# First batch's attention and the first weight tiles in another order: linear attention and a low-rank mixer on one NeuronCore

## The chip, the cores and the metric

The kernel runs on one core of a Trainium2 chip. The metric is the device time of one execution in microseconds (us), the median of five runs. A profile is one more execution, recorded by the hardware profiler; its times are counted from its first instruction. The engines are named as in the profile: PE is TensorE's products, PEld its weight loads, DVE is VectorE, ACT is ScalarE, POOL is GpSimd, SP is the engine that issues the DMAs.

## The reference

Attention with a decaying state, for 4 batches, 8 heads, 768 steps and a head of 48; then a mixer over its output, which mixes the steps through rank 32 and the channels through a two-layer network (384 to 1536 to 384).

```python
f = 1.0 / (1.0 + np.exp(-f_logit))
for t in range(S):
    state = f[:, :, t, :, None] * state + np.einsum('bhd,bhe->bhde', k[:, :, t], v[:, :, t])
    y[:, :, t] = np.einsum('bhd,bhde->bhe', q[:, :, t], state)
...
x = y.transpose(0, 2, 1, 3).reshape(B, S, H * D)
h = x.transpose(0, 2, 1) @ U @ V
u = x + h.transpose(0, 2, 1)
out = u + np.maximum(u @ w_ch1, 0.0) @ w_ch2
```

The weights U, V, w_ch1 and w_ch2 arrive as 64-bit floats, the rest as 32-bit.

## The kernel before

**Units of attention.** A unit is two heads of one batch; there are 16, four to a batch. The sequence of a unit is cut into 12 chunks of 64 steps. `prepare(n)` makes the front of unit n: `gates` (transposes of the forget gates on TensorE into PSUM, L506, and the sigmoid on ScalarE, L527 and L528), `keep` (a backward running product `X` on VectorE, L540, and small follow-ups L545 to L550), `keys` (transposes of k, and `kz` = k times `X`, L518), `read_back` (a forward scan `Y`, L558) and `queries` (the same for q). After each tensor is used, the load of that tensor for unit n + 2 is issued on SP (`follow`, L394).

`attend(n)` makes the rear: `kept` transposes `kz` back (L610) and copies it to `kb` on ScalarE (L614); `states` copies each chunk's whole decay to a broadcast tile `whole` (L618), multiplies `kb` with v into the PSUM tile `ds` (L626) and copies that, interleaved, into `added` (L632); `scan` adds the states up over the chunks on VectorE (L641), in place in `added`, and for batches after the first copies the sums on to a tile `st` (L648); `scores` makes the products of q and k (L589) and masks them into `A` (L596); `read` multiplies q with the states into `y` (L661) and then has ScalarE copy two numbers of it to `seen` (L668), which orders what follows behind it; `inner` adds the products of `A` and v (L679) and copies `y` to `x` (L685). `whole` and `kb` have one buffer each, `st` two, the PSUM tiles of attention share three (`ps_big`).

**The mixer of the first batch.** `low_rank` makes x times U (L146) and a copy `h` (L149); `added_up` sums its four parts (L154) and copies them again (L156); `mix` multiplies with V into `pu` (L171), and VectorE adds the result to x (L161), three additions of 128x768; `turn(a)` transposes a third of x into `put` (L181) and copies it to `uT` (L182). Then `ch1` makes the first layer's products, six groups of 12 records for each pair of weight tiles (`pz`, L193, copied through a Relu at L200); `ch2`, and from the second batch `seven`, the second layer's (L215, L238).

**The weights.** Each tile is loaded raw by SP (L55) and turned from 64 to 32 bits: two copies on ScalarE (L64, L65), three operations on VectorE (L66, L67, L68), one addition on POOL (L69). The list `loads` holds U, two pieces of V (`early` is 3), twelve tiles of w_ch1 and twelve of w_ch2, in this order; the w_ch1 tiles go into `w`, two of them to a pair of `pz` groups.

**What sets the order.** TensorE's instructions stand in the order of the program's calls throughout (L745), VectorE's and ScalarE's as long as the first batch's mixer runs (L746); behind that a planner places those of VectorE and ScalarE, and scans, masks and additions have a high priority there. [...] The four units of batch 0 are written out by hand at L755 to L790. `busy(n)` puts n idle products (L753), whose result nobody reads, into TensorE's list: two at the start, three in each unit, and one before each of the first three pieces of the mixer (`idles`, L780). After the fourth unit's pieces, U and the first piece of V are converted, then unit 3's reading and inner products are done, then V's second piece and the first two tiles of w_ch1. In the mixer one entry of `loads` follows each piece, except the pieces 1 and 2 (`added_up` and `mix`), so the third tile stands behind `low_rank`.

```python
pieces += rear(n - 1, "read") + rear(n, "states", "scan", "scores") + rear(n - 1, "inner")
...
idles = {0: 1, 1: 1, 2: 1}
...
if loads and i not in (1, 2):
    loads.pop(0)()
```

Of the kernel before, what the change touches and what calls it, by code (L numbers as in the profile page):

```python
# [10 lines left out]
F32 = mybir.dt.float32  # L11
# [4 lines left out]
ALU = mybir.AluOpType  # L16
# [307 lines left out]
def factored_path(ctx, tc, q, k, v, f_logit, moe_U, moe_V, moe_w_ch1, moe_w_ch2, out, ok):  # L324
# [4 lines left out]
    nc = tc.nc  # L329
    B, H, S, D = q.shape  # L330
    P = nc.NUM_PARTITIONS
    C = P // 2
    NCH = S // C

    NBL = S // P
    HP = H // 2
# [18 lines left out]
    one = ctx.enter_context(tc.tile_pool(name="one", bufs=1))  # L355
# [215 lines left out]
    def attend(n):  # L571

        b, hp = divmod(n, HP)
        T = units[n]
        vt = v_tiles[n]
        rows = [slice(par * PAD, par * PAD + D) for par in range(2)]
        chunk = [slice(c * C, (c + 1) * C) for c in range(NCH)]

        part = [slice(s * C, (s + 1) * C) for s in range(2)]

        def scores():


            T["A"] = two.tile([P, 2, NBL, C], F32, name="A")
            sc = ps_big.tile([P, 2, 512], F32, name="sc", tag="big")
            for c in range(NBL):
                for par in range(2):
                    for s in range(2):
                        nc.tensor.matmul(  # L589
                            sc[part[s ^ par], par, c * C : (c + 1) * C],  # L590
                            lhsT=T["k"][rows[par], chunk[2 * c + s]],
                            rhs=T["q"][rows[par], chunk[2 * c + s]],
                            start=True, stop=True,
                        )
            with tc.high_priority(offset=AHEAD):
                nc.vector.tensor_tensor(  # L596
                    T["A"],
                    sc[:, :, 0 : NBL * C].rearrange("p h (c i) -> p h c i", i=C),
                    causal.unsqueeze(1).unsqueeze(1).broadcast_to((P, 2, NBL, C)),
                    ALU.mult,  # L600
                )

        def kept():

            pt = ps_big.tile([P, 2, 512], F32, name="pt", tag="big")
            for c in range(NBL):
                for par in range(2):
                    r = slice(par * PAD, (par + 1) * PAD)
                    o = c * P + (1 - par) * C
                    nc.tensor.transpose(  # L610
                        pt[:, par, c * PAD : (c + 1) * PAD], kz[n % 2][r, o : o + P], ident[r, r]
                    )
            kb = T["kb"] = one.tile([P, 2, NBL, PAD], F32, name="kb")
            nc.scalar.copy(kb.rearrange("p h c d -> p h (c d)"), pt[:, :, 0 : NBL * PAD])  # L614

        def states():
            whole = T["whole"] = one.tile([P, D, NCH], F32, name="whole")
            nc.scalar.copy(whole, wholes[n % 2].unsqueeze(1).broadcast_to((P, D, NCH)))  # L618

            ds = ps_big.tile([P, 2, 512], F32, name="ds", tag="big")  # L620
            for c in range(NBL):
                for s in range(2):
                    for par in range(2):

                        i = (c + (s & par)) % NBL
                        nc.tensor.matmul(  # L626
                            ds[par * PAD : (par + 1) * PAD, s, c * D : (c + 1) * D],
                            lhsT=T["kb"][part[s ^ par], par, i, :], rhs=vt[part[s ^ par], c, par, :],
                            start=True, stop=True,
                        )  # L630

            nc.scalar.copy(  # L632
                added[:, 1:].rearrange("p (e c s) -> p e c s", c=NBL, s=2),
                ds[:, :, 0 : NBL * D].rearrange("p s (c e) -> p e c s", e=D),
            )

        def scan():

            states = added[:, 0 : D * NCH]
            with tc.high_priority(offset=AHEAD):  # L640
                nc.vector.tensor_tensor_scan(  # L641
                    states, states, T["whole"].rearrange("p e c -> p (e c)"), 0.0, ALU.add, ALU.mult
                )
                T["st"] = states.rearrange("p (e c) -> p c e", c=NCH)
                if b > 0:

                    st = two.tile([P, NCH, D], F32, name="st")
                    nc.scalar.copy(st, T["st"])  # L648
                    T["st"] = st

        def read():


            y = T["y"] = ps_big.tile([P, 2, 512], F32, name="y", tag="big")

            def o(s, par, c):
                return y[part[s], par, c * D : (c + 1) * D]

            for c in range(1, NCH):
                for par in range(2):  # L660
                    nc.tensor.matmul(  # L661
                        o(c % 2, par, c // 2), lhsT=T["q"][rows[par], chunk[c]], rhs=T["st"][rows[par], c, :],
                        start=(c <= 2), stop=False, skip_group_check=True,
                    )


            seen = two.tile([P, 2], F32, name="seen")
            nc.scalar.copy(seen, y[:, :, (NBL - 1) * D])  # L668

        def inner():  # L670
            y = T["y"]

            def o(s, par, c):
                return y[part[s], par, c * D : (c + 1) * D]

            for c in reversed(range(NBL)):
                for par in range(2):
                    for s in range(2):
                        nc.tensor.matmul(  # L679
                            o(s, par, c), lhsT=T["A"][part[s ^ par], par, c, :], rhs=vt[part[s ^ par], c, par, :],  # L680
                            start=False, stop=True, skip_group_check=True,
                        )
            if hp == 0:
                x_tiles[b] = two.tile([P, NBL, DM], F32, name="x")
            nc.scalar.copy(  # L685
                x_tiles[b].rearrange("p c (h d) -> p h c d", d=D)[:, 2 * hp : 2 * hp + 2],
                y[:, :, 0 : NBL * D].rearrange("p h (c d) -> p h c d", d=D),
            )
            del units[n], v_tiles[n]

        return [kept, states, scan, scores, read, inner]
# [54 lines left out]
    with tc.manual_schedule(engines={nc.vector.engine, nc.scalar.engine}):  # L746


        idle = ps_mm.tile([P, 512], F32, name="idle", tag="mm")

        def busy(n):
            for _ in range(n):
                nc.tensor.matmul(idle[:, 0:DM], lhsT=ident, rhs=ends[:, 0:DM], start=True, stop=True)  # L753

        busy(2)  # L755
        for piece in front(0, "gates"):
            piece()
        for n in range(HP):
            pieces = front(n, "keep", "keys") + rear(n - 1, "scan", "scores")
            pieces += [lambda: busy(3)] + rear(n, "kept") + front(n, "read_back", "queries")  # L760
            if n + 1 < HP:
                pieces += front(n + 1, "gates") + rear(n - 1, "read", "inner") + rear(n, "states")
            else:
                pieces += rear(n - 1, "read") + rear(n, "states", "scan", "scores") + rear(n - 1, "inner")
            for piece in pieces:
                piece()
            if n < 2:
                load(n + 2, "v")
            if n == 1:

                loads = ahead_by(early + FIRST, weights)
            elif n > 1:
                load(n + 2, "f", "k", "q", "v")
        for piece in loads[:2] + rear(HP - 1, "read", "inner") + loads[2 : early + 2]:
            piece()
        loads = loads[early + 2 :]

        m = mixer(0)
        start = m.before[:5] + m.firsts[0:1] + m.before[5:]
        idles = {0: 1, 1: 1, 2: 1}  # L780

        EARLY = 9
        second = chain(front(HP, "gates", "keep", "keys", "read_back", "queries"), steps(HP, 2 * HP + 1))
        for i, (_, piece) in enumerate(start + m.firsts[1:]):
            busy(idles.get(i, 0))
            piece()
            if loads and i not in (1, 2):
                loads.pop(0)()
            if i >= EARLY:
                next(second)()  # L790
        for f in loads:
            f()
        n = len(m.seconds) // (NBL // 2)
        todo, after = m.seconds[:-n], m.seconds[-n:]

        attention(second, 12 + 10 * HP - (len(start) + len(m.firsts) - 1 - EARLY), todo)
        m = start_mixer(1, after)
        for f in to_sum:
            f()
# [343 lines left out]
```

## Time and profile before

| | us |
|---|---|
| median of five runs | 503.35 |
| lowest and highest | 502.57, 505.9 |
| the profiled execution's own time | 503.69 |
| its span, first to last instruction | 501.9 |
| TensorE products busy in it | 485.9 (97%) |
| VectorE, ScalarE, POOL busy | 274.8, 157.2, 37.6 |
| mean granted TensorE clock | 0.992 |

The page of the profile gives each engine's busy time in 40 equal slices of 12.5 us, in tenths:

```profile
PE   6897999999999999999999999999999999999995
DVE  5895989787587757656865436633411431222232
ACT  2424665664333313423332222413311122101010
PEclk9997999999999999999999999999999999999999
```

TensorE is below nine tenths in the first three slices and in the last, and the granted clock is below full in the fourth. The median of a group of instructions, and what an engine waited for, come from the groups and waits of the same trace; a wait marked "issue" is one for which the profile shows no releaser. Where a matmul ends is modelled.

### The profile page before, as it was taken

The numbers are of one execution on the slowest core, as the hardware profiler recorded it, in microseconds if no ns is written. First come the engines' busy times: TensorE is split into PE (matmuls) and PEld (weight loads), VectorE is DVE, ScalarE is ACT, GpSimd is POOL, SyncE is SP. The second block draws the span as 40 slices with busy tenths as digits, with TensorE's granted clock in tenths as the row PEclk, the third lists the DMA queues.
The fourth block names the chain that finished last, engine by engine and source line by source line (L and its number), as shares of the span: only waits on it lengthen the run. The fifth ranks groups of instructions, "written<-read, shape, count | busy, mean of one in ns | idle before, by whom it ended". The sixth has DMA issues, their size and how long they took to land.

```text
span 501.9 us, 12045 instructions
## 1 busy us (share of the span) xinstructions
PE 485.9 (97%) x5319; PEld 405.3 (81%) x5319; DVE 274.8 (55%) x396; ACT 157.2 (31%) x297; POOL 37.6 (7%) x49
## 2 busy tenths in 40 slices
PE   6897999999999999999999999999999999999995
PEld 4676588887666568898898888898899888999995
DVE  5895989787587757656865436633411431222232
ACT  2424665664333313423332222413311122101010
POOL 3000345442000000000000000000000000000000
PEclk9997999999999999999999999999999999999999
DMA  9979977634676422424534100100000000000001
GB/s 145 153 165 241 210 177 174 175 88 62 102 110 102 91 39 28 66 29 88 65 50 80 25 31 3 25 1 34 2 3 31 2 33 1 0 33 0 31 3 39
DMA packets 149269, 34.32 MB, mean 68 GB/s; under 512 B 139798, under 2 KB 147670, under 8 KB 149206
## 3 DMA queue, kind: packets, MB, share of 16 engines
q1 hardware_dynamic: 149206, 33.44, 35.5%
q8 instruction: 44, 0.72, 0.7%
q14 instruction: 19, 0.16, 0.1%
HBM read 28.70 MB, written 4.72 MB: 67 GB/s over the span
## 4 chain that ended last, share of the span: by engine, by line
PE 92%; SPq 3%; DVE 2%; DMA 1%; issue 1%; ACT 0%; ACTq 0%
PE pz L193 38%; PE pw L238 25%; PE po L215 10%; PE y L679 3%; PE y L661 3%; PE pt L506 3%; PE sc L589 3%; PE ds L626 2%; SPq L394 2%; PE put L181 2%; PE pt L610 1%; DMA f_raw<-in_f_logit_dram 1%; PE idle L753 1%; PE pu L171 1%; PE ph L146 1%
## 5 line engine op out<-in xcount | busy, mean ns | idle before, releaser
L193 PE MATMUL pz<-uT,w 128*128 128x256 f32 x864 | 195.8, 382 | 0.1
L193 PEld LDWEIGHTS pz<-uT,w 128*128 128x128 f32 x864 | 161.1, 190 | 22.1 <-issue 0.3
L200 ACT ACTIVATE z<-pz 128x512 f32<-128x512 f32 x63 | 37.6, 596 | 131.7 <-PE pz L193 127.5
L238 PE MATMUL pw<-w,z 128*128 128x192 f32 x324 | 56.5, 329 | 0.4 <-DVE o L161 0.4
L238 PE MATMUL pw<-zw,w_raw 128*128 128x192 f32 x324 | 55.9, 327 | 0.0
L238 PEld LDWEIGHTS pw<-w,z 128*128 128x128 f32 x324 | 52.8, 190 | 2.3 <-DVE o L161 1.6
L238 PEld LDWEIGHTS pw<-zw,w_raw 128*128 128x128 f32 x324 | 53.0, 190 | 1.3 <-DVE o L161 1.2
L161 DVE TENSOR_TENSOR w_raw<-z 128x768 f32<-128x768 f32 x18 | 17.2, 954 | 56.3 <-ACT z L200 56.3
L69 POOL TENSOR_TENSOR w<-w_y,w_r 128x384 int32<-128x384 int32 x24 | 31.5, 1311 | 35.9 <-DVE w_y L68 28.0
L540 DVE TENSOR_TENSOR_SCAN X<-fz,ends 128x768 f32<-128x768 f32 x16 | 28.1, 1756 | 10.5 <-ACT fz L527 6.2
L558 DVE TENSOR_TENSOR_SCAN Y<-fz,starts 128x768 f32<-128x768 f32 x16 | 27.9, 1746 | 0.2
L641 DVE TENSOR_TENSOR_SCAN added<-added,whole 128x576 f32<-128x576 f32 x16 | 21.6, 1352 | 8.8 <-ACT added L632 8.8
L215 PE MATMUL po<-w,zw 128*128 128x384 f32 x72 | 25.6, 499 | 0.0
L215 PE MATMUL po<-w,z 128*128 128x384 f32 x72 | 25.3, 495 | 0.0
L596 DVE TENSOR_TENSOR A<-sc,causal 128x768 f32<-128x768 f32 x16 | 15.2, 947 | 16.9 <-PE sc L589 16.9
L161 DVE TENSOR_TENSOR w_y<-x,pw 128x192 f32<-128x192 f32 x9 | 3.2, 354 | 38.5 <-ACT w_y L251 38.5
L648 ACT COPY st<-added 128x576 f32<-128x576 f32 x12 | 14.7, 1222 | 18.9 <-DVE added L641 18.9
L161 DVE TENSOR_TENSOR w_y<-w_y,pw 128x192 f32<-128x192 f32 x18 | 6.2, 347 | 25.6 <-PE pw L238 25.6
L215 PEld LDWEIGHTS po<-w,zw 128*128 128x128 f32 x72 | 12.9, 189 | 8.7 <-issue 1.2
L614 ACT COPY kb<-pt 128x768 f32<-128x768 f32 x16 | 12.7, 795 | 22.0 <-PE pt L610 22.0
L215 PEld LDWEIGHTS po<-w,z 128*128 128x128 f32 x72 | 13.0, 190 | 8.1 <-DVE o L161 0.6
L66 DVE TENSOR_SCALAR w_y<-w_y 128x384 f32<-128x384 f32 (+3 forms) x27 | 13.1, 484 | 11.6 <-ACT w_y L64 11.4
(102 smaller groups left out, 533.1 us busy)
## 6 DMA issues: line engine op xcount, KB each, us to landing
w_raw<-in_moe_w_ch_dram SPq DMA_DIRECT2D x18, 384.0 KB, 3.6
out_dram<-o SPq DMA_DIRECT2D x24, 192.0 KB, 2.0
f_raw<-in_f_logit_dram SPq DMA_DIRECT2D x16, 144.0 KB, 4.6
k_raw<-in_k_dram SPq DMA_DIRECT2D x16, 144.0 KB, 4.2
q_raw<-in_q_dram SPq DMA_DIRECT2D x16, 144.0 KB, 4.2
v_nat<-in_v_dram SPq DMA_DIRECT2D x16, 144.0 KB, 4.2
v_nat<-in_v_dram SPq DMA_DIRECT2D x32, 72.0 KB, 2.8
zw<-in_moe_w_ch_dram SPq DMA_DIRECT2D x6, 384.0 KB, 7.3
```

The source lines that it names most:

```text
L69: nc.gpsimd.tensor_tensor(dst.bitcast(I32), shaped(y.bitcast(I32)), shaped(r), ALU.add)
L161: nc.vector.tensor_tensor(*args)
L193: nc.tensor.matmul(pm[:, i * 2 * P : (i + 1) * 2 * P], lhsT=w1[:, m, o : o + P], rhs=uT[a][:, m, :], start=(m == 0), stop=(m == NDC - 1))
L200: nc.scalar.activation(z[a, c][:, k : k + 2, :].rearrange("p i t -> p (i t)"), pm, AF.Relu)
L215: nc.tensor.matmul(pm, lhsT=z[a, i // NI][:, i % NI, s * P : (s + 1) * P], rhs=w2[:, i, :], start=(i == 0), stop=(i == NFC - 1))
L238: nc.tensor.matmul(pm[:, n * HM : (n + 1) * HM], lhsT=lhs[:, i, :], rhs=rhs[:, i, :], start=(i == 0), stop=(i == NI - 1))
L506: nc.tensor.transpose(pt[:, 2 * c // NBL, c % (NBL // 2) * P : (c % (NBL // 2) + 1) * P], nat[n % 2][nm][:, c].rearrange("p h d -> p (h d) ...
L540: nc.vector.tensor_tensor_scan(backwards(X, S - 1, S), backwards(f, S, S), backwards(ends, S - 1, S), 0.0, ALU.mult, ALU.add,)
L558: nc.vector.tensor_tensor_scan(Y, f[:, 0:S], starts, 0.0, ALU.mult, ALU.add)
L589: nc.tensor.matmul(sc[part[s ^ par], par, c * C : (c + 1) * C], lhsT=T["k"][rows[par], chunk[2 * c + s]], rhs=T["q"][rows[par], chunk[2 * ...
L596: nc.vector.tensor_tensor(T["A"], sc[:, :, 0 : NBL * C].rearrange("p h (c i) -> p h c i", i=C), causal.unsqueeze(1).unsqueeze(1).broadcast ...
L641: nc.vector.tensor_tensor_scan(states, states, T["whole"].rearrange("p e c -> p (e c)"), 0.0, ALU.add, ALU.mult)
```

## The change

Six edits, all in the part of the program that handles the first batch, except that the order of two copies and the place where `st` is made hold for every unit:

1. One idle product at the start in place of two.
2. The copy to `whole` moves from `states` to `kept`, ahead of the copy to `kb`.
3. In the first batch the scan writes a tile `st` with two buffers instead of writing over `added`; TensorE reads the states from there, with the same strides. Later batches still scan in place and copy to `st`.
4. In the last unit of the first batch `states` comes ahead of the reading of the unit before.
5. Behind it, unit 3's reading comes ahead of the conversion of U and V's first piece.
6. No idle product before `low_rank`; and the third tile of w_ch1 is converted behind `mix` instead of behind `low_rank`.

```diff
                         pt[:, par, c * PAD : (c + 1) * PAD], kz[n % 2][r, o : o + P], ident[r, r]
                     )
+            whole = T["whole"] = one.tile([P, D, NCH], F32, name="whole")
+            nc.scalar.copy(whole, wholes[n % 2].unsqueeze(1).broadcast_to((P, D, NCH)))
             kb = T["kb"] = one.tile([P, 2, NBL, PAD], F32, name="kb")
             nc.scalar.copy(kb.rearrange("p h c d -> p h (c d)"), pt[:, :, 0 : NBL * PAD])
 
         def states():
-            whole = T["whole"] = one.tile([P, D, NCH], F32, name="whole")
-            nc.scalar.copy(whole, wholes[n % 2].unsqueeze(1).broadcast_to((P, D, NCH)))
...
         def scan():
 
-            states = added[:, 0 : D * NCH]
+            st = T["st"] = two.tile([P, NCH, D], F32, name="st")
+            by_e = "p (e c) -> p c e"
+            if b == 0:
+                states = st.rearrange("p c e -> p (c e)")
+                T["st"] = states.rearrange(by_e, c=NCH)
+            else:
+                states = added[:, 0 : D * NCH]
             with tc.high_priority(offset=AHEAD):
                 nc.vector.tensor_tensor_scan(
-                    states, states, T["whole"].rearrange("p e c -> p (e c)"), 0.0, ALU.add, ALU.mult
+                    states, added[:, 0 : D * NCH], T["whole"].rearrange("p e c -> p (e c)"), 0.0, ALU.add, ALU.mult
                 )
-                T["st"] = states.rearrange("p (e c) -> p c e", c=NCH)
                 if b > 0:
 
-                    st = two.tile([P, NCH, D], F32, name="st")
-                    nc.scalar.copy(st, T["st"])
-                    T["st"] = st
+                    nc.scalar.copy(st, states.rearrange(by_e, c=NCH))
...
-        busy(2)
+        busy(1)
...
-                pieces += rear(n - 1, "read") + rear(n, "states", "scan", "scores") + rear(n - 1, "inner")
+                pieces += rear(n, "states") + rear(n - 1, "read") + rear(n, "scan", "scores") + rear(n - 1, "inner")
...
-        for piece in loads[:2] + rear(HP - 1, "read", "inner") + loads[2 : early + 2]:
+        for piece in rear(HP - 1, "read") + loads[:2] + rear(HP - 1, "inner") + loads[2 : early + 2]:
             piece()
...
-        idles = {0: 1, 1: 1, 2: 1}
+        idles = {1: 1, 2: 1}
...
-            if loads and i not in (1, 2):
+            if loads and i > 1:
                 loads.pop(0)()
```

## The prediction

> **What bounds the kernel now.** I read the busy table by stretch first, then the chain of waits, then the timeline of the first 58 us. The stretches (columns: us of the stretch, busy us and instructions of each engine, granted TensorE clock, DMA share, GB/s):
>
> ```profile
> core 0: us, PE busy (x) PEld busy (x) DVE busy (x) ACT busy (x) POOL busy (x), PEclk, DMA share, GB/s
> 0.00:20.05 20.05, 14.43 (x173) 9.85 (x173) 13.74 (x20) 6.35 (x12) 4.66 (x22) 1.00 1.25 152
> 20.05:38.31 18.26, 17.61 (x448) 13.51 (x448) 15.88 (x19) 7.21 (x16) 0.00 (x0) 1.00 0.82 162
> 38.31:42.65 4.34, 2.18 (x105) 2.04 (x105) 2.45 (x3) 1.54 (x4) 0.00 (x0) 1.00 1.06 344
> 42.65:58.00 15.35, 13.59 (x221) 8.60 (x220) 11.33 (x22) 7.30 (x19) 4.47 (x6) 0.78 1.04 165
> 58.00:496.44 438.44, 438.04 (x4375) 371.30 (x4375) 231.07 (x333) 134.84 (x248) 28.49 (x21) 1.00 0.28 55
> ```
>
> From 58 us TensorE is full for 438.04 of 438.44 us. So the change can pay or cost only before its first `pz` product (57.99), and a shift there reaches the end whole. Before it TensorE idles 10 us, under three different limits.
>
> Until 20.05 it is the loads. Unit 2's forget gates land at 19.91, as SP issues 0.4 to 1 us per DMA and the engines are full:
>
> ```profile
> 14.53 5.38 DMA f_raw<-in_f_logit_dram
> ```
>
> Then, 20.05 to 40.5, it is TensorE and VectorE in turn. Then TensorE stops for 2.16 us in the middle of the scores of unit 3, where no semaphore stands ("issue"), and its clock halves:
>
> ```profile
> 42.65 0.86 PE L589 MATMUL sc<-qT,kz 48*64 48x64 f32 x35 [2.16 <-issue]
> ...
> q8 instruction: 1, 0.02, 2.3%
> ...
> 42.60:46.60 4.00, 3.39 (x128) 3.23 (x127) 1.61 (x4) 1.63 (x6) 0.00 (x0) 0.57 1.01 175
> ...
> 43.00:43.50 0.50, 0.50 (x36) 0.50 (x32) 0.00 (x0) 0.00 (x0) 0.00 (x0) 0.63 1.34 227
> ...
> 49.50:50.00 0.50, 0.50 (x5) 0.20 (x8) 0.47 (x3) 0.50 (x2) 0.00 (x0) 0.54 1.19 159
> ```
>
> These are from the timeline, from the DMA queues of the stretch 39.5 to 42.5 (one packet of instructions; in 35.5 to 40 there is none) and from the table by stretch. Its last two lines show the clock leaving 1.00 near 43.1 and returning near 50.0. The rest, to 58, is a thin chain:
>
> ```profile
> 46.42 0.14 ACT L668 COPY seen<-y 128x2 f32<-128x2 f32 x1
> ...
> 46.64 1.53 PE L679 MATMUL y<-v_nat,A 64*64 64x48 f32 x48 [0.59 <-ACT seen L668]
> ...
> 50.53 0.57 ACT L64 ACTIVATE w_y<-zw 128x384 f32<-128x384 f32 x1 [0.34 <-POOL V L69]
> ...
> 51.97 0.91 PE L154 MATMUL ph<-h,blocks 128*128 128x384 f32 x2
> ...
> 52.95 0.55 ACT L65 ACTIVATE w_r<-zw 128x384 int32<-128x384 uint32 x1
> ...
> 53.40 0.47 ACT L156 COPY h<-ph 128x384 f32<-128x384 f32 x1
> ...
> 54.01 1.56 PE L171 MATMUL pu<-h,V 32*128 32x384 f32 x12 [0.48 <-ACT h L156]
> ...
> 54.65 0.56 DVE L68 SCALAR_TENSOR_TENSOR w_y<-zw,w_y 128x384 uint32<-128x384 uint32 x1
> ...
> 55.13 2.67 DVE L161 TENSOR_TENSOR x<-x,pu 128x768 f32<-128x768 f32 x3
> ...
> 56.13 1.74 PE L181 MATMUL put<-ident,x 128*128 128x128 f32 x12 [0.56 <-DVE x L161]
> ```
>
> The third weight tile's VectorE work (L66 to L68, ending 55.21) is what the additions wait for; its ScalarE half (ending 53.50) is what the second `h` copy waits for.
>
> [...]
>
> **The change part by part.**
>
> *Front: one idle product fewer.* Two records at 0.64 us leave the head, so unit 0 starts up to 1.3 us sooner. Unit 2's gates still land at 19.91: worth 0. What it can cost, a clock that rises later than before, is bounded by 1.5 to 2 us of lateness on VectorE, which the 2.16 us stall at 40.49 covers. Without that cover it would reach the end.
>
> *`whole` ahead of `kb`, out of `states`.* 0.67 us of ScalarE moves, 16 times; none added. In units 1 and 2 the scan started when VectorE had finished `kz` (24.78 + 0.96, scan at 25.66), not when `added` came: gain 0. Unit 1's `whole` must now wait for scan 0 (ends 17.81), so `kb` goes from 18.11 to 18.5; `ds` needs it at 23.06: hidden. In later batches `kb` (85.59) leads `ds` (96.49) by 10 us: 0.
>
> *Scan into `st`, unit 3's states ahead of unit 2's reading.* Products and strides are the same. `ds` can run at about 38.5 (`kb` ends 38.48), `added` ends about 40.1, the scan starts about 1 us sooner than 41.04. But reading unit 3 (44.48) stands behind the rest of the scores[...], and behind unit 2's inner products. Instruction counts ahead of the stall change by four, SP's and POOL's lists keep their order, so I leave the fetch where it is: gain 0. Its bounds: 0, if the stall stays; about 2 us, if it went.
>
> *`seen` ahead of U's and V's copies.* Reading ends at 46.04, `seen` ran at 46.42, after four weight copies (45.47 to 46.51). Now it runs at once and L679 may start at 46.30 instead of 46.64: 0 to 0.34 us[...]. I take 0.2. Queued behind it now are the four copies (1.04 us, done by 47.4, before `x` at 48) and VectorE's five instructions for U and V (45.88 to 47.98, 2.1 us), which end near 48.85, just when V's second piece comes (49.12 − 0.2): cover with nothing over.
>
> *Idle product before `low_rank` gone.* 1.65 us of TensorE (48.10 to 49.75) go; `low_rank` starts at 48.7, not 49.68. But the first `h` copy (51.46) stands behind the second tile's L64, which waits for POOL's V: it moves by the 0.2 only. Gain 0.
>
> *Third tile behind the additions.* ScalarE: L64 and L65 leave the front of L156. The product of L154 ends at 51.97 + 0.91 = 52.88, the copy starts there, 0.47 + 0.14 to the next product, so `pu` at 53.5 (its idle pair ends at 53.53), with the 0.2 at 53.33. VectorE: 53.18 to 55.21 leaves the front of the additions; VectorE is free at 53.06. Batch 1 shows from first `pu` to first addition 0.96 us where VectorE was idle:
>
> ```profile
> 178.11 1.56 PE L171 MATMUL pu<-h,V 32*128 32x384 f32 x12
> ...
> 179.07 2.68 DVE L161 TENSOR_TENSOR x<-x,pu 128x768 f32<-128x768 f32 x3 [5.08 <-PE pu L171]
> ```
>
> So the additions start at 53.33 + 0.96 = 54.29 instead of 55.13: 0.84 us sooner, no longer bound by VectorE but by TensorE and the copy. The third tile is then converted from 54.29 + 2.67 = 56.96 and stored by POOL near 59.3 (before, 56.35). It is needed by the fourth `pz` group, at about 57.15 + 2.83 + 0.66 + 2 × 2.6 = 65.8: hidden with 6 us over. No load is moved: SP's order is the same.
>
> Sum: 0.2 + 0.64 = 0.84 us. Against the profiled execution (503.69: span 501.87 and 1.8 around it) 502.85. The median of the five runs is 503.35, 0.3 lower, so I forecast 502.5.
>
> **The rivals.** *The clock stays down (slower).* [...] `pu` near 55.4 and at half speed, additions near 57.1, a loss of 2 us, 505.3. It decides once `pu` starts after 54.17. [...] Against: at the head 2.9 us of large products (2.74 to 5.67) brought it up, from records 0.64 us apart there to 0.37 at 15.3.
>
> *The clock never drops or the stall shrinks (faster by more).* [...] With the clock full, inner products of unit 3 run 0.86 us in place of 1.53[...]: 0.85 instead of 0.2, total 1.5, 501.9. If the 2 us stall went as well, `x` would be ready near 46.0 instead of 48.9: 2.9 + 0.64 = 3.5, 499.8. Against: the weights fill the DMA engines just as before.
>
> *Nothing happens:* `pu` held by its idle pair and V's conversion behind U's; 503.2.
>
> **How the numbers follow.** Forecast 45% (501.8 to 503.0); clock down longer 25% (503.6 to 505.3); clock or stall better 22% (499.8 to 501.9); nothing 8%. The range that leaves out 2 in 10: 500.5 to 504.4. One measurement of this kernel cannot tell 0.5% (2.5 us) from no change; the five runs spread over 3.3 us. Over that bound: faster needs most of the stall to go, 0.14; [...] within, 0.77.
>
> **What would show it.** Right: additions L161 near 54.3 with TensorE's `pu` as their releaser, first `pz` near 57.15, the stall at the scores still about 2 us. Wrong: clock at 0.5 past 50.0; `pu` later than 54.1; no stall near 40.6; a `pz` group waiting for POOL between 60 and 70; or TensorE with gaps after 58, which would undo the carry to the end.

## The result, and the profile after

| | before | after |
|---|---|---|
| median, us | 503.35 (79 runs, 501.98 to 506.91) | 505.23 (42 runs, 502.94 to 507.91) |
| ratio | | 1.0035 [1.0027, 1.0044] |
| profiled execution, its span | 503.69, 501.9 | 505.69, 504.0 |
| first `pz` product | 57.99 | 59.99 |

The change costs 0.35%, 1.9 us. The forecast was 502.5 with 500.5 to 504.4: the sign came out the other way, and the time lies above the range. The table by stretch of the kernel after (columns as in the prediction):

```profile
core 0: us, PE busy (x) PEld busy (x) DVE busy (x) ACT busy (x) POOL busy (x), PEclk, DMA share, GB/s
0.00:20.05 20.05, 15.80 (x170) 10.65 (x170) 12.92 (x20) 7.11 (x13) 4.67 (x22) 1.00 1.23 150
20.05:38.31 18.26, 17.40 (x452) 13.61 (x454) 16.48 (x19) 7.80 (x17) 0.00 (x0) 1.00 0.82 169
38.31:42.65 4.34, 2.13 (x106) 1.99 (x107) 2.57 (x3) 0.80 (x2) 0.00 (x0) 1.00 1.07 333
42.65:58.00 15.35, 12.08 (x204) 7.34 (x203) 7.74 (x18) 6.54 (x17) 3.48 (x5) 0.67 0.96 159
58.00:496.44 438.44, 437.81 (x4375) 370.70 (x4376) 233.81 (x337) 136.03 (x249) 29.47 (x22) 1.00 0.27 54
```

Three readings. TensorE is as full behind 58 us as before (437.81 of 438.44), so the 2.0 us by which the first `pz` comes later are the whole loss of this execution. Up to 38.31 nothing is lost: 170 + 452 products are done, 173 + 448 before. All of it happens between 38.31 and 58, and from 42.65 on TensorE's clock averages 0.67 instead of 0.78. (In the page of the profile before, the slices below nine tenths are the first, the second and the fourth, not the first three; the fourth, 37.6 to 50.2 us, holds this stall.) The timeline of that stretch:

```profile
43.62 0.74 PE L589 MATMUL sc<-qT,kz 48*64 48x64 f32 x34 [3.18 <-issue]
...
47.97 1.53 PE L682 MATMUL y<-v_nat,A 64*64 64x48 f32 x47 [0.91 <-issue]
...
49.56 0.64 ACT L688 COPY x<-y 128x576 f32<-128x576 f32 x1 [1.94 <-PE y L682]
...
50.34 2.77 PE L146 MATMUL ph<-x,U 128*32 128x384 f32 x12 [0.84 <-ACT x L688]
...
53.05 1.65 PE L756 MATMUL idle<-ends,ident 128*128 128x384 f32 x2
...
54.49 1.02 PE L154 MATMUL ph<-h,blocks 128*128 128x384 f32 x2
...
55.54 0.48 ACT L156 COPY h<-ph 128x384 f32<-128x384 f32 x1 [1.91 <-PE ph L154]
...
56.16 1.56 PE L171 MATMUL pu<-h,V 32*128 32x384 f32 x12
...
57.12 2.68 DVE L161 TENSOR_TENSOR x<-x,pu 128x768 f32<-128x768 f32 x3 [2.54 <-PE pu L171]
...
59.99 1.32 PE L193 MATMUL pz<-uT,w 128*128 128x256 f32 x5
```

Four lines of before that the prediction doesn't show:

```profile
48.24 0.64 ACT L685 COPY x<-y 128x576 f32<-128x576 f32 x1 [1.68 <-PE y L679]
...
49.68 1.60 PE L146 MATMUL ph<-x,U 128*32 128x384 f32 x12
...
51.21 0.91 PE L753 MATMUL idle<-ends,ident 128*128 128x384 f32 x2
...
57.99 2.83 PE L193 MATMUL pz<-uT,w 128*128 128x256 f32 x12
```

Read them together with those of the prediction. The stall in the scores lasts 3.18 us instead of 2.16 and ends at 43.62 instead of 42.65. A second one, also without a releaser, stands at unit 3's inner products (0.91), so they start at 47.97 instead of 46.64 and the last copy to `x` at 49.56 instead of 48.24. From there the chain runs at half clock: twelve `low_rank` products take 2.77 us (1.60 before), two idle ones 1.65 (0.91 before). The additions come at 57.12 (55.13 before).

The packet of instructions shows in the DMA queues. Between 36.5 and 41 us there is only the loads' queue (packets, MB, share):

```profile
q1 hardware_dynamic: 1504, 1.49, 102.1%
```

and between 39.5 and 43.5 the one packet appears, whose record runs from 41.16 to 42.21 (before: 40.11 to 41.20):

```profile
q8 instruction: 1, 0.02, 1.6%
```

Start and end are those of the packet's own record in the trace, which the view doesn't print. TensorE goes on 1.4 us behind the end (before: 1.5). That it waits for this packet, called the fetch below, is read from the order of the times alone, as the stall has no releaser.

The clock, from the table by stretch (third number from the end of a line):

```profile
44.50:45.00 0.50, 0.50 (x40) 0.50 (x34) 0.50 (x1) 0.00 (x0) 0.00 (x0) 0.66 1.12 224
54.50:55.00 0.50, 0.50 (x2) 0.33 (x1) 0.08 (x1) 0.00 (x0) 0.28 (x1) 0.60 1.43 175
55.00:55.50 0.50, 0.50 (x3) 0.35 (x2) 0.00 (x0) 0.00 (x0) 0.50 (x1) 1.00 1.37 157
```

0.66 over half a us means a drop at 44.66, 0.60 a return at 54.90, from full to half clock (0.50) and back. That makes 10.24 us of half clock, where before it was 6.83 (43.13 to 49.96).

One profile is one draw, though. Each run also lists its mean clock. As the low clock is 0.50 in both traces, the time spent there is 2 × (1 − mean) × span: 8 us for before's 0.992 (its trace has 6.83, and 1.4 at the end) and 12 for 0.988 after (10.24, and 2.0 at the end). The mean doesn't count the time before the clock's rise, in the first 12 us. So 0.997 and above stands for about 3 us of half clock or less, 0.991 to 0.996 for 4 to 9, 0.990 and below for 10 or more; the three profiled executions of the first group (e4, h2, k1) had none between the rise and the last 5 us. (Runs, median us:)

| | 0.997 and above | 0.991 to 0.996 | 0.990 and below |
|---|---|---|---|
| before (263 runs, those of the experiments) | 69, 502.76 | 148, 503.43 | 46, 505.09 |
| after (44, the profiled one among them) | 0 | 7, 503.68 | 37, 505.68 |

With the shares of after and the medians of before one gets (7 × 503.43 + 37 × 505.09) / 44 = 504.83, with before's own shares 503.54. So 1.3 of the 1.9 us go with the time at half clock. This is a correlation: a run with more of it may also have had a longer stall. What brought it is for the experiments.

### The profile page after: what moved, and what is told of

Its sections match the earlier page's. It is cut to its first block, busy times and chain, and to the rows that moved or that the text cites. A ratio compares the mean times of both kernels' runs of the same rounds, so it can differ in the third digit from the quotient of the medians.

```text
span 504.0 us, 12038 instructions
## 1 busy us (share of the span) xinstructions
PE 487.4 (97%) x5315; PEld 406.1 (81%) x5315; DVE 274.7 (55%) x396; ACT 158.3 (31%) x297; POOL 37.6 (7%) x49
## 4 chain that ended last, share of the span: by engine, by line
PE 95%; DMA 2%; issue 1%; DVE 1%; SPq 0%; ACT 0%; ACTq 0%
PE pz L193 38%; PE pw L238 25%; PE po L215 10%; PE pt L506 3%; PE y L682 3%; PE y L664 3%; PE ds L626 3%; PE sc L589 2%; PE idle L756 2%; PE put L181 2%; PE pt L610 2%; PE ph L146 1%; PE pu L171 1%; DMA f_raw<-in_f_logit_dram 1%; DMA k_raw<-in_k_dram 1%
## 5 line engine op out<-in xcount | busy, mean ns | idle before, releaser
L161 DVE TENSOR_TENSOR w_y<-x,pw 128x192 f32<-128x192 f32 x9 | 3.2, 354 | 38.5 <-ACT w_y L251 38.5
L647 DVE TENSOR_TENSOR_SCAN added<-added,whole 128x576 f32<-128x576 f32 x12 | 16.2, 1353 | 7.3 <-ACT added L632 7.3
L238 PE MATMUL pw<-w,w_raw 128*128 128x192 f32 x108 | 19.2, 328 | 0.0
L682 PEld LDWEIGHTS y<-v_nat,A 64*64 64x64 f32 x768 | 13.7, 141 | 6.0 <-issue 4.2
```

Source lines behind the costliest of these rows:

```text
L161: nc.vector.tensor_tensor(*args)
L238: nc.tensor.matmul(pm[:, n * HM : (n + 1) * HM], lhsT=lhs[:, i, :], rhs=rhs[:, i, :], start=(i == 0), stop=(i == NI - 1))
L647: nc.vector.tensor_tensor_scan(states, added[:, 0 : D * NCH], T["whole"].rearrange("p e c -> p (e c)"), 0.0, ALU.add, ALU.mult)
L682: nc.tensor.matmul(o(s, par, c), lhsT=T["A"][part[s ^ par], par, c, :], rhs=vt[part[s ^ par], c, par, :], start=False, stop=True, skip_gro ...
```

## The experiments

All kernels were timed in five rounds beside the kernel before, whose medians in the five sets were 503.34 to 503.6. A ratio is to the kernel before, with its 95% interval; it isn't the quotient of the two medians, and can differ from it by 0.15% (e2).

**First set: putting the idle products back.** Theory A: the idle product missing before `low_rank` keeps the clock down. Theory B: the one missing at the start makes everything late, and the fetch meets more loads. Theory C: the edits of order cost by themselves. Edits to the changed kernel (e3 has both):

```diff
-        busy(1)
+        busy(2)
...
-        idles = {1: 1, 2: 1}
+        idles = {0: 1, 1: 1, 2: 1}
```

> The changed kernel with two idle products at the start again; everything else as changed. Theory A (the idle product before low_rank decides[...]): this stays slow, near 505, clock at half for about 10 us behind the stall, additions near 57. Theory B (the missing idle product at the start decides: the clock rises later, unit 2 runs 0.2 to 0.35 us late, the instruction fetch meets more weights and the stall is 3.2 instead of 2.2 us): about 1.3 us come back, near 503.9, and the stall is near 2.2 us again.

> The changed kernel with the idle product before low_rank again; one at the start as changed. Theory A: [...] low_rank's end to pu shrinks by about 1.4 us, near 503.7. Theory B: the stall is still near 3.2 us and the time stays near 504.8.

> The changed kernel with both idle products again, so only the edits of order remain. If the idle products are the whole loss (theories A and B together) this is faster than the kernel before by what the prediction gave the order edits, 0.6 to 0.8 us: near 502.6. Theory C (the order edits themselves cost[...]): still above 504.

And the kernel before with the third tile's edit alone:

```diff
-            if loads and i not in (1, 2):
+            if loads and i > 1:
```

> The kernel before with one edit alone: the third weight tile behind the additions. The prediction's arithmetic gives 0.64 us, near 502.7, additions starting near 54.5 with TensorE as their releaser. Theory C: no gain, as another wait takes its place, 503.3 or above.

| | us (runs) | ratio |
|---|---|---|
| e1, start restored | 504.68 (14) | 1.0023 [1.0001, 1.0046] |
| e2, `low_rank` restored | 504.15 (14) | 0.9996 [0.9976, 1.0016] |
| e3, both restored | 505.03 (14) | 1.0021 [1.0000, 1.0041] |
| e4, third tile only | 503.31 (22) | 0.9991 [0.9974, 1.0007] |

e2 by itself fits theory A: it is level with the kernel before. But e3, which has that idle product too, is 0.9 us slower than e2, though the two intervals overlap. With both idle products back, most of the loss is still there, so A and B don't carry it alone; the next set decides. The third tile loses nothing. What e3 has beyond e4 are the edits of order.

**Second set: order alone, idle products alone, and fewer early loads.** f3 is the kernel before with edits 2 to 5, f4 with edit 1 and the first half of edit 6. f1 (before) and f2 (after) try to get the loads out of the fetch's way:

```diff
-                loads = ahead_by(early + FIRST, weights)
+                loads = ahead_by(early + 2, weights)
```

> The kernel before, with two instead of six weight tiles loaded ahead of unit 4's inputs (the other four are asked for one at a time, from 45 us on). Theory F (the block of instructions that TensorE misses at the scores is fetched behind the weight loads in the DMA engines[...]): [...] the stall at L589 falls from 2.2 to under 0.5 us, [...] and the median goes from 503.5 to about 500.5. Rival (the stall has another cause, or weights 3 to 6 come late): the stall stays at 2 us or more and the median at 503 to 505.

> The changed kernel with the same two weight tiles loaded early. Theory F: the change loses through the longer stall, so with the stall gone it is no slower than the kernel before with the same edit: 500.0 to 500.8, stall under 0.5 us. Theory A (the missing idle products keep the clock down whatever the stall): [...] it is 1.5 to 2 us above its partner, 502 or more.

> The kernel before with the three edits of order alone: the copy of whole ahead of kb, the sums of states of unit 3 ahead of unit 2's reading with the scan writing st, and seen ahead of the copies for U and V. Both idle products and the third tile stay as before. Theory C (these edits cost by themselves, by a later fetch of instructions): about 505, 1.5 us over the kernel before, with a stall at the scores of 2.7 us or more[...]. Theories A and B (only the idle products matter): 503.5, as the kernel before, stall near 2.2 us.

> The kernel before with the two idle products cut (one at the start, one ahead of low_rank) and nothing else of the change. Theories A and B: about 505[...]. Theory C: 503.5, the same as the kernel before, and a share of runs without half clock (about one in three) as it has.

| | us (runs) | ratio |
|---|---|---|
| f1, before, two tiles early | 506.34 (8) | 1.0056 [1.0032, 1.0079] |
| f2, after, two tiles early | 503.75 (22) | 0.9997 [0.9982, 1.0011] |
| f3, order only | 505.19 (17) | 1.0039 [1.0022, 1.0056] |
| f4, idle cuts only | 503.6 (22) | 1.0014 [0.9999, 1.0030] |

f3, with both idle products, has the whole loss. f4 leaves a small one that the interval doesn't separate from none, but none of its 22 runs had a mean clock of 0.997 or more, where a quarter of the kernel before's have. f1 and f2 failed as tests of the fetch: SP, with four loads fewer to issue, asked for unit 4's inputs at 33.65 instead of 37.98, so they took the weights' place. In f1 TensorE then stopped at another place, also without a releaser (2.42 us, from 36.9 on).

**Third set: which of the order edits, and a first pause in SP's list.** g3 is edit 5 alone, g4 edits 2, 3 and 4. g1 (before) and g2 (after) hold the fourth weight tile's load back until unit 3's `A` is there, by a copy that the load must wait for:

```diff
+            nc.gpsimd.tensor_copy(raw.bitcast(F32)[:, 0:1], hold.pop())
...
-                loads = ahead_by(early + FIRST, weights)
-            elif n > 1:
-                load(n + 2, "f", "k", "q", "v")
+                for start, _ in weights[: early + SOON]:
+                    start()
+            elif n == HP - 1:
+                hold.append(held["A"][:, 0, 0, 0:1])
+                loads = ahead_by(early + FIRST, weights, early + SOON)
+                for i in range(HP, HP + 2):
+                    load(i, "f", "k", "q", "v")
```

> The kernel before with a pause in SP's list: three weight tiles are asked for early as before, then the other three and the inputs of units 4 and 5 only once unit 3's scores have been masked (a one-column copy by POOL from A into the fourth tile makes the transfer wait; the tile is overwritten by the load). Theory F (a block of instructions is fetched only when the loads ahead have drained, whatever they carry): with nothing new in the DMA engines from about 37 us, the packet of instructions[...] starts by 38.5 instead of 40.1, the stall at the scores is under 0.5 us, the next at the inner products of unit 3 too, the third copy of x comes near 46 instead of 48.2, half clock before 58 us becomes rare and the median is 500 to 501.5. Rival (the stall isn't the loads', or the late loads bind: weight tiles 4 to 6 and unit 4's inputs are needed from 60 us on): 503.3 or more, with waits for zw or for unit 4's loads after 58 us.

> The changed kernel with the same pause in SP's list. Theory F (the order edits lose because the block is fetched later): its loss goes, it stands level with the kernel before with the pause or up to 0.6 us ahead of it (third tile): 499.5 to 501.5. Theory C2 (the order edits cost on the engines, without the fetch): it stays 1.3 to 1.9 us above that kernel.

> The kernel before with one of the order edits: seen of unit 3 ahead of the copies for U and V. If it carries the 1.85 us that the three order edits cost together: 505.1; TensorE's and VectorE's lists are unchanged by it. If not: 503.3, as the kernel before, or up to 0.3 less.

> The kernel before with the other two order edits: whole ahead of kb with the scan writing st, and the sums of states of unit 3 ahead of unit 2's reading. If they carry the 1.85 us: 505.1, with a stall at the scores of 2.4 us or more. If not: 503.3.

| | us (runs) | ratio |
|---|---|---|
| g1, before, pause | 503.48 (14) | 1.0007 [0.9989, 1.0025] |
| g2, after, pause | 505.0 (22) | 1.0027 [1.0011, 1.0042] |
| g3, `seen` only | 503.58 (14) | 0.9996 [0.9981, 1.0012] |
| g4, states only | 504.98 (22) | 1.0027 [1.0015, 1.0040] |

The loss lies in edits 2 to 4. The pause didn't come about: the planner, which places SP's instructions, moved the held load to 51 us and let the others pass it, so g1 and g2 say nothing on the fetch.

**Fourth set: the line, and a real pause.** h3 is g4 with one line as before, so it keeps `whole` and `st`:

```diff
-                pieces += rear(n, "states") + rear(n - 1, "read") + rear(n, "scan", "scores") + rear(n - 1, "inner")
+                pieces += rear(n - 1, "read") + rear(n, "states", "scan", "scores") + rear(n - 1, "inner")
```

h1 (before) and h2 (after) are g1 and g2 with SP's list in the written order:

```diff
-    with tc.manual_schedule(engines={nc.vector.engine, nc.scalar.engine}):
+    with tc.manual_schedule(engines={nc.vector.engine, nc.scalar.engine, nc.sync.engine}):
```

> The kernel before with the pause of g1 and SP's list in the written order, so that now everything behind the third weight tile (three weight tiles, the inputs of units 4 and 5, later weights) really waits for unit 3's masked scores. Theory F: the packet of instructions[...] starts by 38.5, the stalls at the scores and at unit 3's inner products fall under 0.5 us each, x(3) is copied near 46, runs without half clock before 58 us go from one in five to most, and the median is 500 to 501.5. Rival F0 (the block comes late for another reason than loads): the packet still starts after 39.5 us with the DMA engines quiet, stall 2 us, 503.4. Rival L (late loads bind): no stall, but waits for f_raw or weights after 58 us, 502.5 or more.

> The changed kernel with the same. Theory F: the states edit loses only through the fetch and the clock, so it ends level with h1 or up to 0.6 us ahead: 499.5 to 501.5. Theory C2 (the edit costs on the engines): 1.3 us or more above h1.

> The kernel before with whole ahead of kb and the scan writing st, but unit 3's sums of states behind unit 2's reading, as before. If the order of unit 3's pieces is what costs: 503.4, the fetch for the scores near 40.0 us and the stall's end near 42.5[...]. If whole or st cost: 505.0, the fetch near 41.0 and the end near 43.3[...].

| | us (runs) | ratio |
|---|---|---|
| h1, before, quiet queue | 507.71 (16) | 1.0069 [1.0048, 1.0089] |
| h2, after, quiet queue | 504.7 (22) | 1.0017 [1.0000, 1.0034] |
| h3, `whole` and `st` only | 503.34 (22) | 0.9989 [0.9974, 1.0005] |

h3 against g4 puts the loss on one line, edit 4: unit 3's states ahead of unit 2's reading, 504.98 − 503.34 = 1.6 us of the 1.9. The timelines of g4 and h3 at the stall and at the first `pz`:

```profile
43.14 0.74 PE L589 MATMUL sc<-qT,kz 48*64 48x64 f32 x35 [2.74 <-issue]
...
58.50 2.83 PE L193 MATMUL pz<-uT,w 128*128 128x256 f32 x12
```

```profile
42.11 0.74 PE L589 MATMUL sc<-qT,kz 48*64 48x64 f32 x35 [1.36 <-issue]
...
57.53 2.83 PE L193 MATMUL pz<-uT,w 128*128 128x256 f32 x12
```

The stall ends 1.0 us later with the states ahead, and so does the rest. This isn't the luck of two profiles. Of the twelve profiled kernels that ask for six weight tiles early, the six with the edit (after, e1, e2, e3, f3, g4) end the stall at 43.13 to 44.00 and have the packet of instructions at 40.60 to 41.52; the six without it (before, e4, f4, g3, h3, k3) at 41.33 to 42.97 and 38.64 to 40.55. The groups don't overlap, and their means are 1.15 us (43.50 and 42.35) and 1.24 us (41.04 and 39.80) apart. This delay and the 1.3 us that go with the time at half clock aren't to be added up: they are two views of one loss, and no run separates them.

h2's timeline shows what a quiet queue does, and what it cost here:

```profile
44.78 0.91 PE L686 MATMUL y<-v_nat,A 64*64 64x48 f32 x47 [0.63 <-issue]
...
52.13 2.68 DVE L161 TENSOR_TENSOR x<-x,pu 128x768 f32<-128x768 f32 x3 [1.21 <-PE pu L171]
...
54.99 2.83 PE L193 MATMUL pz<-uT,w 128*128 128x256 f32 x12
...
65.90 0.55 ACT L64 ACTIVATE w_y<-w_raw 128x384 f32<-128x384 f32 x1 [5.01 <-DMA w_raw<-in_moe_w_ch_dram]
...
67.52 2.83 PE L193 MATMUL pz<-uT,w 128*128 128x256 f32 x12 [3.72 <-ACT z L200]
```

The stall in the scores is nearly gone (0.16 us), the clock is never halved before the end, and the first `pz` comes at 54.99, 5.0 us sooner than in the changed kernel. Then 3.72 us are lost to the seventh weight tile, whose load stood behind unit 5's inputs: ScalarE waits 5.01 us for it, and `z`, for which TensorE waits, stands behind it in ScalarE's list. Rival L of the expectation held for the time. Theory F held for the stall in part: in h1 it is 1.08 us, and the packet starts at 39.08, later than the 38.5 that I expected. The three tiles that are still asked for early fill the DMA engines until then (share 0.93 from 38.5 to 39, 0.35 in the next half us). There the packet starts as the loads drain. But e4, whose engines stayed full (share 1.00 from 36.5 to 38.5, 1.04 in the next us), has it at 38.64, as early as the quiet kernels, so the loads aren't shown to be the whole of the wait.

**Last set: the weights in front, and the one line undone.** k1 and k2 are h1 and h2 with the loads in another order (k2 shown):

```diff
+        fetch = [lambda i=i: load(i, "f", "k", "q", "v") for i in range(HP, HP + 2)]
-        for piece in rear(HP - 1, "read") + loads[:2] + rear(HP - 1, "inner") + loads[2 : early + 2]:
+        for piece in (
+            rear(HP - 1, "read") + loads[:1] + fetch[:1] + loads[1:2] + rear(HP - 1, "inner")
+            + loads[2 : early + 1] + fetch[1:] + loads[early + 1 : early + 2]
+        ):
```

k3 is the changed kernel with h3's line.

> h1 with the seventh weight tile's load ahead of unit 4's inputs and the next three ahead of unit 5's, which in h1 came behind both (TensorE waited 3.7 us at 64 us for them). Theory F: the stalls stay as short as in h1 (1.3 and 1.2 us, none with luck), first pz near 55.7 as in h1, no wait for weights at 64 us, so 2.3 us of the kernel before's 57.99 are kept: 500.5 to 501.5. Rival: the loads collide elsewhere (unit 4's inputs late near 70 us): 503 or more.

> The changed kernel with the same. Theory F: first pz near 55.0 as in h2, against 59.99 in the changed kernel, so 499.8 to 500.8, below both kernels and 0.5 to 1 us below k1 by the third tile; unit 3's states ahead of the reading cost nothing once the fetch is on time. Theory C2 (they cost on the engines): at or above k1.

> The changed kernel with one line put back: unit 3's states behind unit 2's reading. If that line is the loss, as g4 (1.0027) against h3 (0.9989) says: 503.4, 1.8 us under the changed kernel, fetch for the scores near 40 us, some runs without half clock. If the loss is spread over the parts: 504.5 or more.

| | us (runs) | ratio |
|---|---|---|
| k1, before, quiet, weights first | 501.65 (15) | 0.9966 [0.9953, 0.9979] |
| k2, after, quiet, weights first | 501.25 (22) | 0.9969 [0.9950, 0.9988] |
| k3, after, unit 3's order restored | 504.18 (14) | 1.0014 [0.9995, 1.0033] |

k1 and k2 are faster than both kernels, each a little slower than I expected. k1's table by stretch, to be held against that of before in the prediction:

```profile
38.31:42.65 4.34, 3.81 (x189) 3.50 (x190) 2.64 (x3) 1.97 (x4) 0.00 (x0) 1.00 0.33 100
42.65:56.00 13.35, 10.56 (x154) 5.97 (x146) 11.40 (x23) 7.47 (x19) 4.66 (x7) 1.00 0.85 196
```

With the DMA engines at 0.33 instead of 1.06, TensorE makes 189 products between 38.31 and 42.65 instead of 105, and the clock stays at 1.00 to 56. Twelve of k1's 15 runs and twelve of k2's 22 had a mean clock of 0.997 or more. Among those, k2 (500.82) is 0.8 us ahead of k1 (501.65). Over all runs the two ratios are level: with the fetch earlier, the change as a whole costs nothing that can be measured, where it costs 0.35% otherwise. Edit 4 alone was not tried there. k2's profiled execution was none of the twelve (504.36, first `pz` at 58.64): its clock fell already at 22.3.

k3 gives back 1.05 of the 1.9 us, less than I expected. Its ratio is that of the idle cuts alone (f4, 1.0014), and like f4 it had no run at 0.997 or more. So the rest of the loss agrees with the two idle products, but neither interval excludes none.

## Why the prediction was wrong

**The step that failed** is "Scan into `st`, unit 3's states ahead of unit 2's reading". It said "I leave the fetch where it is: gain 0", with bounds of "0, if the stall stays; about 2 us, if it went", both on the side of a gain. The side that came true had no bound: the fetch could come later. Measured: the stall's end 1.15 us later over six kernels each, the time 1.6 us longer (g4 against h3). That TensorE counts almost the same instructions and SP keeps its list was true, but it was no reason for the fetch to stay where it was.

The path from there, in the two profiles: the stall ends later, `x` is ready later (49.56 against 48.24), the clock falls 1.5 us later (44.66 against 43.13) and is still halved when `low_rank`, L154 and the idle pair run. Where the clock falls differs from run to run (in e1, which has the line too, at 42.65), so that part is one draw. The quiet queue supports the link: with fewer loads in front of the fetch the stall is 0.16 to 1.08 us (h1, h2, k1), and in k1 and k2 the half clock becomes rarer and the change's cost is gone. In h1 and h2 it doesn't become rare (1 of 16 and 6 of 22 runs at 0.997 or more); in h1's profile the clock falls at 69.2, behind the wait for the weights. What is not shown is why this order makes the packet start later. The loads don't differ: unit 4's gates are asked for at 38.09 in the mean of the six kernels with the edit and at 38.14 in the six without. That stays open.

**The rival "the clock stays down"** had the size: with the clock down through `pu` it gave additions near 57.1 and 505.3; they came at 57.12, and 505.23 was measured. That it fits so well is luck. How long the clock would stay down was my estimate, which no trace of before shows. It had `pu` near 55.4 at half speed; the clock was back at 54.90, and `pu` came at 56.16 at full speed (1.56 us for the twelve, as before), behind a stall that ended later. Its cause was only a part. I put it down to the idle product missing before `low_rank`; with that restored the time is 504.15 (e2), with both 505.03 (e3), and cut alone the two cost 0.14% [−0.01, 0.30] (f4). What the rival lacked was the later stall, which I had treated as a separate case that can only help.

**Front, one idle product fewer: 0.** Neither shown right nor wrong, but the risk that it names came true: the clock rises later. The first transposes of before and after:

```profile
5.46 0.88 PE L506 MATMUL pt<-ident,f_raw 128*128 128x128 f32 x6
```

```profile
4.81 1.51 PE L506 MATMUL pt<-ident,f_raw 128*128 128x128 f32 x6 [0.43 <-DMA f_raw<-in_f_logit_dram]
```

Unit 0 starts 0.65 us sooner, not 1.3, and loses it again, as its products take almost twice as long. (The tables by stretch print 1.00 there; the durations say otherwise.) In the traces of all kernels the clock's first record of full speed stands at 5.58 to 8.89 us in the twelve with two idle products at the start, and at 8.26 to 11.21 in the eight with one. Unit 2's gates landed at 20.11, 0.2 later; the 3 us stall covers that in the profile. What it does to the clock later on is open: f4 and k3 have no run at 0.997 or more, but k2 and h2, which also start with one idle product, have twelve and six of 22.

**`whole` and `st`: 0.** Agrees (h3, 0.9989 [0.9974, 1.0005]).

**`seen` ahead of the copies: 0.2.** Too small to tell (g3, 0.9996 [0.9981, 1.0012]).

**Third tile: 0.64.** Agrees. The additions start 0.96 us after `pu` with TensorE as their releaser, as worked out from batch 1, and no `pz` group waits for POOL; e4's ratio 0.9991 [0.9974, 1.0007] allows 0.64 us and doesn't prove it, and k2 against k1 at full clock, 0.8, compares the whole change.

**The carry to the end.** Right: 2.0 us at the first `pz`, 2.0 in the profiled executions.

## What to carry to other kernels

A stall without a releaser at a fixed place in TensorE's list is a resource like any other: bound it on both sides for every edit, even one that moves no instruction past it, and look at what fills the DMA engines while the packet of instructions is due (here the stall was 0.16 us in h2 and 3.18 in the changed kernel). A clock that is halved for 6.83 us in one execution (before), 10.24 in another (after) and not before the end in a third (k1) makes the time a mixture: compare the shares of runs by mean clock, not two profiles. And check a pause or a reordering in the trace before reading its time, as four of the kernels here (f1, f2, g1, g2) had other loads move into the gap.

## What the runs showed that I had not expected

The kernel before is itself a mixture: a quarter of its runs (69 of 263) had a mean clock of 0.997 or more, about 3 us of half clock or less, and the medians of the three groups are 502.76, 503.43 and 505.09. The prediction treated the half clock from 43.1 to 50.0 as a property of the kernel.

With the DMA engines full (share 1.06 before, 1.07 after, from 38.31 to 42.65), the packet of instructions started at 38.64 (e4) to 41.52 us in the twelve kernels with six early tiles, and TensorE started again 1.3 to 1.6 us after the packet's end (42.65 after 41.20 before; 41.33 after 39.80 in e4). Fewer weight tiles early didn't prevent a stall: in f1, with two of them and unit 4's inputs close behind, TensorE stopped for 2.42 us.

Spacing the loads was worth more than any edit of the change: 1.7 us (k1).
